# Attention scores of two heads at a time on the two row halves of the TensorE array

## The chip, the cores and the metric

One NeuronCore of one Trainium2 chip runs the kernel. The metric is the device time of one execution in microseconds (us); for the kernel before, three runs are given, and one more execution that the hardware profiler recorded.

## The reference

Attention with capped scores over 4 batches of 12 heads, 448 positions and 64 elements a head, then two blocks of dense products over the 1792 tokens.

```python
scale = 1.0 / np.sqrt(q.shape[-1])
scores = scale * np.matmul(q, k.transpose(0, 1, 3, 2))
scores = cap * np.tanh(scores / cap)
scores = scores - np.max(scores, axis=-1, keepdims=True)
attn = np.exp(scores)
attn = attn / (np.sum(attn, axis=-1, keepdims=True) + 1e-09)
attn_out = np.matmul(attn, v)
...
h = x @ w_in                      # 1792 x 768 x 2048
g = h * np.cos(h)
x = g @ w_out
a = x @ w1; b = x @ w2            # 768 x 1024
return ((a * b) @ w3) @ w_out2
```

## The kernel before, in words

The whole program is recorded first as a list of operations with due times (class `Plan`), and a planner then writes out every engine's order: at each moment it gives a free engine the ready operation with the earliest due time, by the costs that each operation names and the buffers that are free (`Ring`). The due times come from the table `PAR` (L294). What the planner sets is the order; on the chip the engines wait for one another by semaphores.

There are two copies of the program. The first, `columns` (L666), is the one that runs here; the other one (`general=True`) is entered only if the cap is over 40, and is not run with these inputs.

**Numbers in two parts.** Most products are made of values that are split into a high part and a low part of the type float32r, and three products (high by high, high by low, low by high; `mm3`, L380) are added in PSUM. A split is a cast for the high part and a subtraction for the low part (`copy` and `lo`).

**Scores.** Heads are taken in order, 48 of them, in steps `g`; a head has two steps (NT = 2), each for two of its four chunks of 112 keys, so there are 96 steps. For a pair of heads, `a_load` (L526) sends q and k of the two heads, each 64 rows by 2 × 448 columns, to SBUF twice: once to the upper 64 partitions and once to the lower 64. `a_split` (L540) makes from them `qh` and `ql` (high and low part of q, each on both halves of the partitions) and `ks`, whose upper 64 partitions hold the high part of k and whose lower 64 hold the low part. `c_S` (L605) then contracts over 128 rows: `ks` by `qh` (L612) and `ks` by `ql` (L613) give all four products of the parts with two matmuls a chunk. A step has four such matmuls of 448 columns, with weights of 112 columns, and fills the two banks of one `double`, of which there are two.

**The rest of attention.** `c_exp` (L617) takes tanh and exp of both banks in two ScalarE instructions a step. `c_PV` (L625) multiplies the result `p` by v in plain float32 (L633, each matmul shown as two instructions), with a half of the weights set to one so that the sums come out of the same product. `c_move`, `c_sums`, `c_norm` and `a_out` move, normalize and split the output.

**What stands around it.** While the scores go on, TensorE is given other products by due time: first `make_w34` (the product of w3 and w_out2, L381 to L383 on `w2h`, `w3h` and so on), then the units of the first dense block, `moe1` (on `xh`, `wih`, `g`, `woh`). After some 490 us no score products are left, and `moe1` and `moe2` fill the rest.

**Queues.** All DMAs are issued by SyncE (SP) in the planner's order. The first ones are the cap, q and k of the first pair, raw weights of w3 and w_out2, and v.

Of the kernel before, what the change touches and what calls it, by code (L numbers as in the profile page):

```python
# [11 lines left out]
F32 = mybir.dt.float32  # L12
F32R = mybir.dt.float32r
# [6 lines left out]
P = 128  # L20
B, H, S, D = 4, 12, 448, 64
CP = 112
NC = S // CP
# [6 lines left out]
NH = B * H  # L30
# [6 lines left out]
PAD = 64  # L37
# [97 lines left out]
class Plan:  # L135
# [156 lines left out]


PAR = dict(  # L294
    p1=3.4, p2=6.2, gsw=48, t0=10.0,
    ql=6, qs=3,
    hsw=27,
    wb=(20.0, 90.0), we=(90.5, 170.5), e1=2.6, e2=15.1, e3=20.0,
    m0=184.3, ua=14, pa=21.4, pu=14.75,
    wlead=3.1,  # L300


    wACT=1.0, wDVE=1.0, wPOOL=1.0, tw=432.21, back=1.13,
    nq=1, nqh=2, nph=2, npl=2,
    nraw=3, nx=2, w3bufs=2, w2bufs=6,
)
# [1 line left out]
    p1=1.98, p2=2.86, gsw=90, t0=14.13, ql=10, qs=4, hsw=26, wb=(30.36, 107.61), we=(108.65, 207.54),  # L308
    m0=222.0, ua=13, pa=19.15, pu=14.2, nt=9, nph=3,
# [22 lines left out]
def program(  # L332
# [15 lines left out]
    PE, ACT, DVE, POOL, SP = nc.tensor, nc.scalar, nc.vector, nc.gpsimd, nc.sync  # L348
    G = dict(PAR, **GENERAL) if general else PAR
    plan = Plan()  # L350
# [4 lines left out]
    def copy(due, dst, src, n, on, psum=False):  # L355
        opts = {
            "A": ("ACT", (0.051 if psum else 0.094) + n / 1200, lambda: ACT.copy(dst(), src())),  # L357
            "D": ("DVE", 0.068 + n / (960 if psum else 1920), lambda: DVE.tensor_copy(dst(), src()))  # L358
            + (() if psum else (True,)),
            "P": ("POOL", 0.16 + n / 1200,  # L360
                  lambda: POOL.tensor_scalar(dst(), src(), 1.0, 0.0, op0=ALU.mult, op1=ALU.add)),
        }
        plan.op(due, [opts[e] for e in on], r=[src], w=[dst])

    def tt(due, dst, a, b, n, op, on="D", psum=False):
        opts = {
            "D": ("DVE", 0.068 + n / 960, lambda: DVE.tensor_tensor(dst(), a(), b(), op=op))  # L367
            + (() if psum else (True,)),
            "P": ("POOL", 0.158 + n / 480, lambda: POOL.tensor_tensor(dst(), a(), b(), op=op)),
        }  # L370
        plan.op(due, [opts[e] for e in on], r=[a, b], w=[dst])

    def lo(due, dst, src, hi, n, on="PD", psum=False):
        tt(due, dst, src, hi.view(lambda t: t.bitcast(F32)), n, ALU.subtract, on, psum)

    def dma(due, dst, src, r=(), w=(), kb=115, write=False):
        plan.op(due, [("SP", 0.66, lambda: SP.dma_start(dst(), src()))], r=r, w=w,  # L377
                kb=kb)
# [6 lines left out]
    MM = (S + 32) / 2400  # L385
# [10 lines left out]
    for name, kw in dict(const={}, xring={}, dram=dict(space=DRAM), psum=dict(space=PSUM), doubles=dict(space=PSUM), singles=dict(space=PSUM), attn={}, lp={},  # L396
                         wi=dict(side="right"), wp=dict(side="right"), yp=right, hp=right, mp=right, cv=right,
                         q2=right).items():
# [17 lines left out]
    class Scratch:  # L416
# [7 lines left out]
        def at(self, sub, pick=None):  # L424
            return Ref(self.item, sub, pick)
# [31 lines left out]
    if general:  # L457
        s_r, pt_r, pv_r, hy_r = Banks((0, 1)), Banks((2, 3)), Banks((4, 5)), Banks((6, 7))
    else:
        s_r, pv_r, hy_r = Doubles((0, 1)), Banks((4, 5)), Banks((6, 7))  # L460
# [14 lines left out]
    if general:  # L475
# [18 lines left out]
    xl_r = ring("xring", "xl", [P, KD, S], F32R, 2)  # L494
    xh, xl = {}, {}
    A = {}
    tiles = [
        ("qr", [P, 2, S], F32, G["nq"]), ("kr", [P, 2, S], F32, G["nq"]), ("qh", [P, 2, S], F32R, G["nqh"]),
        ("ql", [P, 2, S], F32R, G["nqh"]), ("ks", [P, 2, S], F32R, G["nqh"]), 
        ("x32", [P, S], F32, 1), ("xsh", [P, S], F32R, 1), ("xsl", [P, S], F32R, 1),  # L500
    ]
    if general:
        tiles += [
            ("vr", [CP, NC, D], F32, 2), ("vs", [CP, NC, 2, D], F32R, 3), ("t", [CP, S], F32, G["nt"]), ("sm", [CP, 2, NC], F32, 4),
            ("rs", [CP, 2, NC], F32, 3), ("rb", [P, S], F32, 1),
            ("ph", [CP, S], F32R, G["nph"]), ("pl", [CP, S], F32R, G["npl"]),
        ]
    else:
        tiles += [(f"v{j}", [CP, NC, 2, D], F32, 2) for j in range(2)]
        tiles += [("p", [CP, 2, S], F32, 3), ("xs", [P, S], F32, 4), ("rs", [P, S // D], F32, 2), ("rb", [P, S], F32, 1)]  # L510
    for tag, shape, dtype, n in tiles:
        A[tag] = ring("attn", tag, shape, dtype, n)

# [4 lines left out]
    qk, vt, st, sm, rs, rb, s_t, t_t, pt_t, ph_t, pv_t, x32 = ({} for _ in range(12))  # L518

    def rows(j):  # L520
        return lambda t: t[j * D:(j + 1) * D]
# [4 lines left out]
    def a_load(i, g):  # L526
        b, h = divmod(i, H)
        qk[i] = A["qr"].new(), A["kr"].new()
        for it, src in zip(qk[i], (q2, k2)):
            for j in range(2):  # L530
                r = it.at(j, rows(j))
                dma(at(g) if i else -99.0, r, lambda src=src: src[b, h // 2].rearrange("(i d) s -> d i s", i=2),
                    w=[r], kb=230)
# [6 lines left out]
    def a_split(i, g):  # L540
        q, k = (Ref(x) for x in qk.pop(i))
        qh, ql, ks = (A[x].ref() for x in ("qh", "ql", "ks"))
        copy(at(g), ks, k, 2 * S, "PAD")
        low = Ref(ks.item, None, rows(1))
        lo(at(g), low, k.view(rows(1)), low, 2 * S)
        copy(at(g), qh, q, 2 * S, "PAD")
        lo(at(g), ql, q, qh, 2 * S)
        for j in range(2):
            st[i + j] = qh[:, j], ql[:, j], ks[:, j]
# [23 lines left out]
    def of_head(f, lag, g, n):  # L573
        i, c = divmod(g - lag, n)
        if c == 0 and 0 <= i < NH:
            f(i, g)

    def of_pair(f, lag, g, n):
        i, c = divmod(g - lag, n)
        if c == 0 and 0 < i < NH and i % 2 == 0:  # L580
            f(i, g)

    def each(f, lag, g, n):
        if 0 <= g - lag < n * NH:
            f(*divmod(g - lag, n), g)
# [4 lines left out]

    NT = NC // 2

    def c_consts():
        for j in range(2):
            r = A[f"v{j}"]
            for _, k in r.free:
                POOL.memset(r.tile(k)[:, :, 1 - j, :], 1.0)
# [4 lines left out]
        vt[i] = A[f"v{j}"].ref()  # L602
        dma(at(g), vt[i][:, :, j, :], lambda: v[b, h], w=[vt[i]])

    def c_S(i, c, g):  # L605
        qh, ql, ks = st[i]
        s = s_t[i, c] = s_r.ref()

        def f():
            for n in range(2):  # L610
                o, w = s()[:CP, n, :S], ks()[:, (2 * c + n) * CP:(2 * c + n + 1) * CP]
                PE.matmul(o, w, qh(), start=True, stop=False)  # L612
                PE.matmul(o, w, ql(), start=False, stop=True)  # L613

        plan.op(at(g), [("PE", 4 * MM, f)], r=st[i], w=[s])

    def c_exp(i, c, g):  # L617
        s = s_t.pop((i, c))[:CP, :, :S]
        p = ph_t[i, c] = A["p"].ref()
        for f, x, o in ((AF.Tanh, ts, s), (AF.Exp, pac, p)):  # L620
            plan.op(at(g), [("ACT", 0.144 + 2 * S / 1200,
                             lambda f=f, x=x, o=o: ACT.activation(o(), s(), f, scale=x[:CP]))],  # L622
                    r=[s], w=[o], table="exp")

    def c_PV(i, c, g):  # L625
        p = ph_t.pop((i, c))
        if c == 0:
            pv_t[i] = pv_r.ref()
        pv, w = pv_t[i], vt[i]

        def f():
            for n in range(2):
                PE.matmul(pv()[:, :S], w()[:, 2 * c + n].rearrange("p a d -> p (a d)"), p()[:, n, :],  # L633
                          start=c == 0 and n == 0, stop=c == NT - 1 and n == 1)

        plan.op(at(g), [("PE", 8 * MM, f)], r=[w, p], w=[pv])

    def c_move(i, g):
        pv, pv_t[i] = pv_t[i], A["xs"].ref()
# [25 lines left out]

    def columns():  # L666
        c_consts()
        a_load(0, -2)
        a_split(0, -1)
        for g in range(-8, NT * NH + 16):  # L670
            of_pair(a_load, -G["ql"], g, NT)
            of_head(cv_load, -2, g, NT)
            of_pair(a_split, -G["qs"], g, NT)
            each(c_S, 0, g, NT)
            each(c_exp, 0, g, NT)
            each(c_PV, 2, g, NT)
            of_head(c_move, 4, g, NT)
            of_head(c_sums, 4, g, NT)
            of_head(c_norm, 8, g, NT)
            of_head(a_out, 9, g, NT)  # L680
            if g == NT * G["hsw"] + 4:
                plan.move(pv_r, hy_r, at(g))
        first = plan.move(s_r, hy_r, at(g), lambda k: ())
        plan.move(s_r, hy_r, at(g), lambda k: range(4), part_doubles, [first])
        plan.move(pv_r, hy_r, at(g))
# [593 lines left out]


    (queries if general else columns)()
    first = make_w34()
    moe2(moe1(*first))
# [50 lines left out]
```

## Time and profile before

| | |
|---|---|
| three runs | 1100.07, 1101.58, 1103.51 us |
| the profiled execution | 1101.39 us |
| its span, first to last instruction | 1099.6 us |
| matmul instructions | 5040 |
| VectorE, share of the span | 80% |
| ScalarE | 46% |
| GpSimd | 14% |
| DMA, mean over the span | 154 GB/s |

The span is what the profile's times are counted from and in; 1.8 us of the execution lie around it. A busy share is an average over stages that have different limits, and a matmul's recorded end is a model, so what a matmul costs is read from the starts of the matmuls after it.

### The profile page before, as it was taken

Reading aid. Unit: us, or ns where it says so; the run is one execution under the profiler, and the core shown is the slowest. Engines: PE = TensorE matmul, PEld = TensorE weight load, DVE = VectorE, ACT = ScalarE, POOL = GpSimd, SP = SyncE. Lnnn points to the kernel's source line nnn. Section 1 sums busy time; section 2 is a strip of 40 time slices with the busy share of each in tenths; the row PEclk is TensorE's granted clock in tenths of the full one; section 3 lists DMA queues with packets and bytes.
Section 4 is the critical chain, followed back from the end, with each engine's and each line's share of the span. In section 5 each row is a group of like instructions: output and inputs, shape, how many; then the busy total and the mean of one; then the engine's idle time right before and its main releaser. Section 6 shows DMA issues by size and latency. Waiting matters only on the chain.

```text
span 1099.6 us, 14038 instructions
## 1 busy us (share of the span) xinstructions
PE 1075.0 (98%) x5040; PEld 938.1 (85%) x5040; DVE 882.5 (80%) x1338; ACT 505.2 (46%) x663; POOL 157.2 (14%) x153
## 2 busy tenths in 40 slices
PE   5999999999999999999999999999999999999996
PEld 3777777778888888889999999998999999999996
DVE  6897758698899989868789977779899879667642
ACT  4887667787666566642244221113333236321121
POOL 2232120131331301101001200001223100000000
PEclk9999999999999999999999999999999999999998
DMA  8885875868756654525643521103655436321132
GB/s 234 222 216 157 226 203 158 227 202 235 199 168 204 173 179 145 176 83 183 226 157 95 165 63 58 58 15 121 234 187 201 143 102 228 113 88 58 58 108 82
DMA packets 95554, 169.04 MB, mean 154 GB/s; under 512 B 37362, under 2 KB 68850, under 8 KB 95474
## 3 DMA queue, kind: packets, MB, share of 16 engines
q1 hardware_dynamic: 95474, 168.05, 51.0%
q8 instruction: 41, 0.67, 0.3%
q14 instruction: 39, 0.32, 0.1%
HBM read 129.30 MB, written 38.62 MB: 153 GB/s over the span
## 4 chain that ended last, share of the span: by engine, by line
PE 83%; DVE 8%; DMA 5%; issue 1%; SPq 1%; POOL 0%; ACT 0%; DVEq 0%; POOLq 0%; ACTq 0%
PE bank L383 23%; PE bank L382 23%; PE bank L381 23%; PE bank L633 9%; PE double L613 2%; PE double L612 2%; DMA raw<-in_w_out 2%; DMA kr<-in_k 1%; DMA rb<-rs_d 1%; SPq L377 1%; DVE x L854 1%; DVE y L367 1%; DMA rs_d<-rs 1%; DVE w L367 1%; DVE x L858 1%
## 5 line engine op out<-in xcount | busy, mean ns | idle before, releaser
L633 PE MATMUL bank<-p,v 112*128 112x448 f32 x384 | 161.1, 542 | 0.4 <-issue 0.4
L381 PE MATMUL bank<-xh,wih 128*128 128x448 f32 x384 | 148.4, 387 | 0.0
L381 PE MATMUL bank<-g,woh 128*128 128x448 f32 x384 | 145.7, 380 | 0.9 <-DVE y L358 0.9
L382 PE MATMUL bank<-g,woh 128*128 128x448 f32 x384 | 139.2, 363 | 0.9 <-DVE g L367 0.9
L382 PE MATMUL bank<-xl,wih 128*128 128x448 f32 x384 | 139.3, 363 | 0.0
L383 PE MATMUL bank<-g,wol 128*128 128x448 f32 x384 | 139.3, 363 | 0.0
L383 PE MATMUL bank<-xh,wil 128*128 128x448 f32 x384 | 139.2, 363 | 0.0
L367 DVE TENSOR_TENSOR y<-bank,y 128x448 f32<-128x448 f32 x168 | 103.7, 619 | 43.5 <-PE bank L383 42.5
L357 ACT COPY hs<-bank 128x448 f32<-128x448 f32 x83 | 44.3, 534 | 199.0 <-PE bank L383 198.8
L622 ACT ACTIVATE double<-double,ts 112x896 f32<-112x896 f32 x96 | 94.0, 980 | 66.3 <-PE double L613 66.0
L633 PEld LDWEIGHTS bank<-p,v 112*128 112x128 f32 x384 | 72.5, 190 | 40.8 <-issue 38.1
L622 ACT ACTIVATE p<-double,pac 112x896 f32<-112x896 f32 x96 | 96.8, 1011 | 2.1
L612 PE MATMUL double<-qh,ks 128*112 128x448 f32 x192 | 73.7, 384 | 14.0 <-DVE ks L367 10.0
L382 PEld LDWEIGHTS bank<-xl,wih 128*128 128x128 f32 x384 | 72.2, 188 | 10.5 <-issue 5.2
L382 PEld LDWEIGHTS bank<-g,woh 128*128 128x128 f32 x384 | 72.1, 188 | 10.0 <-issue 3.7
L381 PEld LDWEIGHTS bank<-g,woh 128*128 128x128 f32 x384 | 71.9, 187 | 10.1 <-issue 2.4
L381 PEld LDWEIGHTS bank<-xh,wih 128*128 128x128 f32 x384 | 72.0, 187 | 9.9 <-issue 4.7
L383 PEld LDWEIGHTS bank<-g,wol 128*128 128x128 f32 x384 | 72.1, 188 | 4.3
L383 PEld LDWEIGHTS bank<-xh,wil 128*128 128x128 f32 x384 | 72.0, 188 | 4.3
L613 PE MATMUL double<-ql,ks 128*112 128x448 f32 x192 | 72.0, 375 | 0.0
L382 PE MATMUL bank<-ab,w34h 128*128 128x448 f32 x192 | 69.7, 363 | 0.0
L381 PE MATMUL bank<-ab,w34h 128*128 128x448 f32 x192 | 69.7, 363 | 0.0
(219 smaller groups left out, 2313.3 us busy)
## 6 DMA issues: line engine op xcount, KB each, us to landing
rawc<-in_w_out SPq DMA_DIRECT2D x16, 768.0 KB, 5.5
stq<-w_d SPq DMA_DIRECT2D x32, 384.0 KB, 3.7
qr<-in_q SPq DMA_DIRECT2D x48, 224.0 KB, 4.7
kr<-in_k SPq DMA_DIRECT2D x48, 224.0 KB, 4.7
rawc<-in_w_in SPq DMA_DIRECT2D x13, 768.0 KB, 5.8
raw<-in_w3T SPq DMA_DIRECT2D x16, 512.0 KB, 5.6
rawl<-in_w SPq DMA_DIRECT2D x10, 768.0 KB, 4.9
raw<-in_w_out SPq DMA_DIRECT2D x8, 768.0 KB, 7.0
```

What stands on the lines that cost most here:

```text
L357: "A": ("ACT", (0.051 if psum else 0.094) + n / 1200, lambda: ACT.copy(dst(), src())),
L367: "D": ("DVE", 0.068 + n / 960, lambda: DVE.tensor_tensor(dst(), a(), b(), op=op))
L377: plan.op(due, [("SP", 0.66, lambda: SP.dma_start(dst(), src()))], r=r, w=w, kb=kb)
L381: PE.matmul(out, wh, xh, start=first, stop=False, skip_group_check=on)
L382: PE.matmul(out, wh, xl, start=False, stop=False, skip_group_check=on)
L383: PE.matmul(out, wl, xh, start=False, stop=last, skip_group_check=on)
L612: PE.matmul(o, w, qh(), start=True, stop=False)
L613: PE.matmul(o, w, ql(), start=False, stop=True)
L622: lambda f=f, x=x, o=o: ACT.activation(o(), s(), f, scale=x[:CP]))],
L633: PE.matmul(pv()[:, :S], w()[:, 2 * c + n].rearrange("p a d -> p (a d)"), p()[:, n, :], start=c == 0 and n == 0, stop=c == NT - 1 and n == 1)
L854: DVE.scalar_tensor_tensor(xi, h_(), 3, xi, op0=ALU.logical_shift_left, op1=ALU.bitwise_or)
L858: DVE.scalar_tensor_tensor(xi, l_(), 29, xi, op0=ALU.logical_shift_right, op1=ALU.bitwise_or)
```

## The change

For a pair of heads, q and k are now loaded once (`c_load`): head 0 of the pair stands on partitions 0 to 63, head 1 on 64 to 127, 448 columns each. `c_split` makes `kh`, `kl`, `qh` and `ql`, each of 128 partitions by 448 columns. A step is now one chunk of 112 keys for both heads: for each of three products (high by high, high by low, low by high) a matmul of 64 rows for head 0 and one for head 1, so six a step, where the fourth product (low by low) is no longer made. Head 0 writes the first bank of a `double`, head 1 the second. `c_PV` takes two chunks of one head from two tiles `p`, of which there are now six. The due times in `PAR` move.

```diff
 PAR = dict(
-    p1=3.4, p2=6.2, gsw=48, t0=10.0,
+    p1=3.2, p2=6.0, gsw=48, t0=7.5,
...
-    wb=(20.0, 90.0), we=(90.5, 170.5), e1=2.6, e2=15.1, e3=20.0,
-    m0=184.3, ua=14, pa=21.4, pu=14.75,
+    wb=(18.0, 83.0), we=(83.5, 158.5), e1=2.6, e2=15.1, e3=20.0,
+    m0=172.2, ua=14, pa=20.7, pu=14.75,
...
-    wACT=1.0, wDVE=1.0, wPOOL=1.0, tw=432.21, back=1.13,
+    wACT=1.0, wDVE=1.0, wPOOL=1.0, tw=410.0, back=1.13,
...
-        tiles += [("p", [CP, 2, S], F32, 3), ("xs", [P, S], F32, 4), ("rs", [P, S // D], F32, 2), ("rb", [P, S], F32, 1)]
+        tiles += [(x, [P, S], F32, G["nq"]) for x in ("qr", "kr")]
+        tiles += [(x, [P, S], F32R, G["nqh"]) for x in ("qh", "ql", "kh", "kl")]
+        tiles += [("p", [CP, 2, S], F32, 6), ("xs", [P, S], F32, 4), ("rs", [P, S // D], F32, 2), ("rb", [P, S], F32, 1)]
...
+    def c_load(i, g):
+        b, h = divmod(i, H)
+        qk[i] = A["qr"].ref(), A["kr"].ref()
+        for r, src in zip(qk[i], (q2, k2)):
+            dma(at(g) if i else -99.0, r, lambda src=src: src[b, h // 2], w=[r], kb=230)
+
+    def c_split(i, g):
+        st[i // 2] = []
+        for src, names in zip(reversed(qk.pop(i)), (("kh", "kl"), ("qh", "ql"))):
+            hi, low = (A[x].ref() for x in names)
+            copy(at(g), hi, src, S, "PAD")
+            lo(at(g), low, src, hi, S)
+            st[i // 2] += [hi, low]
...
-    def c_S(i, c, g):
-        qh, ql, ks = st[i]
-        s = s_t[i, c] = s_r.ref()
+    def c_S(n, c, g):
+        kh, kl, qh, ql = st[n]
+        s = s_t[n, c] = s_r.ref()
+        terms = (kh, qh), (kh, ql), (kl, qh)
 
         def f():
-            for n in range(2):
-                o, w = s()[:CP, n, :S], ks()[:, (2 * c + n) * CP:(2 * c + n + 1) * CP]
-                PE.matmul(o, w, qh(), start=True, stop=False)
-                PE.matmul(o, w, ql(), start=False, stop=True)
-
-        plan.op(at(g), [("PE", 4 * MM, f)], r=st[i], w=[s])
+            for k, (w, x) in enumerate(terms):
+                for j in range(2):
+                    r = slice(j * D, (j + 1) * D)
+                    PE.matmul(s()[:CP, j, :S], w()[r, c * CP:(c + 1) * CP], x()[r], start=k == 0, stop=k == 2)
+
+        plan.op(at(g), [("PE", 3 * MM, f)], r=st[n], w=[s])
...
-    def c_PV(i, c, g):
-        p = ph_t.pop((i, c))
-        if c == 0:
+    def c_PV(i, k, g):
+        n, j = divmod(i, 2)
+        ps = [ph_t[n, c] for c in (2 * k, 2 * k + 1)]
+        if k == 0:
             pv_t[i] = pv_r.ref()
         pv, w = pv_t[i], vt[i]
 
         def f():
-            for n in range(2):
-                PE.matmul(pv()[:, :S], w()[:, 2 * c + n].rearrange("p a d -> p (a d)"), p()[:, n, :],
-                          start=c == 0 and n == 0, stop=c == NT - 1 and n == 1)
+            for c, p in enumerate(ps):
+                PE.matmul(pv()[:, :S], w()[:, 2 * k + c].rearrange("p a d -> p (a d)"), p()[:, j, :],
+                          start=k == 0 and c == 0, stop=k == NT - 1 and c == 1)
...
-            each(c_PV, 2, g, NT)
-            of_head(c_move, 4, g, NT)
-            of_head(c_sums, 4, g, NT)
-            of_head(c_norm, 8, g, NT)
-            of_head(a_out, 9, g, NT)
+            if 0 <= g - 3 < NT * NH:
+                c_PV(*divmod(g - 3, NT), g)
+            of_head(c_move, 5, g, NT)
+            of_head(c_sums, 5, g, NT)
+            of_head(c_norm, 9, g, NT)
+            of_head(a_out, 10, g, NT)
```

The planner's orders show what moves. On TensorE, a step of the scores in the middle of `make_w34`; names are tiles with their buffer numbers, `bank_75` to `bank_78` are PSUM banks, and "x2" marks two instructions alike in a row. Before:

```order
L383 MATMUL bank_78<-w2h_261,w3l_175 128x384
L612 MATMUL double_82<-qh_128,ks_135 112x448
L613 MATMUL double_82<-ql_131,ks_135 112x448
L612 MATMUL double_82<-qh_128,ks_135 112x448
L613 MATMUL double_82<-ql_131,ks_135 112x448
L633 MATMUL bank_75<-p_161,v_107 128x448 x2
L381 MATMUL bank_78<-w2h_286,w3h_163 128x384
```

and in the changed kernel:

```order
L383 MATMUL bank_77<-w2h_298,w3l_172 128x384
L628 MATMUL double_82<-qh_127,kh_132 112x448 x2
L628 MATMUL double_82<-ql_129,kh_132 112x448 x2
L628 MATMUL double_82<-qh_127,kl_135 112x448 x2
L649 MATMUL bank_76<-p_157,v_113 128x448
L649 MATMUL bank_76<-p_170,v_113 128x448
L381 MATMUL bank_78<-w2h_266,w3h_161 128x384
```

Four matmuls of a step have become six, two (one a head) in each row that ends with "x2", and the neighbours are of the same kinds. In both orders the score products stand in 91 unbroken runs, 89 of one step, one of three steps and one, at the very start, of four, with other products before and behind each.

On VectorE, the splits ahead of the first score product. Before:

```order
L358 CAST qh_128<-qr_115 128x896
L367 TENSOR_TENSOR ql_131<-qr_115,qh_128 128x896
L358 CAST ks_135<-kr_118 128x896
L367 TENSOR_TENSOR ks_135<-kr_118,ks_135 64x896
L854 SCALAR_TENSOR_TENSOR x_147<-raw_121,x_147 128x512
```

and in the changed kernel:

```order
L358 CAST qh_127<-qr_115 128x448
L367 TENSOR_TENSOR ql_129<-qr_115,qh_127 128x448
L358 CAST kh_132<-kr_117 128x448
L367 TENSOR_TENSOR kl_135<-kr_117,kh_132 128x448
L873 SCALAR_TENSOR_TENSOR x_153<-raw_119,x_153 128x512
```

The same four instructions stand there in the same order, with half of the columns; the one that made the low part of k on 64 partitions now makes it on 128.

## Rows read from the trace of the kernel before

**Rows 1.** The page, part 1: busy time (share of the span) and instructions.
```profile
PE 1075.0 (98%) x5040; PEld 938.1 (85%) x5040; DVE 882.5 (80%) x1338; ACT 505.2 (46%) x663; POOL 157.2 (14%) x153
```

**Rows 2.** Windows: length, busy us of each engine (instructions), TensorE clock, DMA share, GB/s.
```profile
0.00:20.00 20.00, 8.01 (x20) 5.58 (x20) 11.81 (x17) 8.24 (x10) 6.32 (x13) 1.00 0.94 232
20.00:170.00 150.00, 147.52 (x632) 113.18 (x632) 115.60 (x164) 112.24 (x143) 31.60 (x34) 0.99 0.76 201
170.00:320.00 150.00, 149.09 (x646) 118.67 (x645) 130.70 (x182) 108.28 (x128) 33.72 (x28) 1.00 0.72 200
320.00:470.00 150.00, 150.00 (x667) 123.90 (x666) 134.38 (x199) 96.19 (x106) 26.71 (x25) 1.00 0.58 179
```

**Rows 3.** Waits of TensorE: total us, times, longest us.
```profile
PE double L612 <- DVE ks L367: 10.0, 1, 10.0
PE double L612 <- ACT p L622: 4.1, 2, 2.1
PE bank L382 <- DVE g L367: 0.9, 1, 0.9
PE bank L381 <- DVE y L358: 0.9, 1, 0.9
```

**Rows 4.** Groups of instructions, score matmuls: busy us, mean ns, idle before.
```profile
L612 PE MATMUL double<-qh,ks 128*112 128x448 f32 x192 | 73.7, 384 | 14.0 <-DVE ks L367 10.0
L613 PE MATMUL double<-ql,ks 128*112 128x448 f32 x192 | 72.0, 375 | 0.0
```

**Rows 5.** Timeline, TensorE matmuls, 298.5 to 301 us: start, length, instruction.
```profile
298.73 0.36 PE L612 MATMUL double<-qh,ks 128*112 128x448 f32 x1
...
299.33 0.37 PE L613 MATMUL double<-ql,ks 128*112 128x448 f32 x1
299.54 1.67 PE L633 MATMUL bank<-p,v 112*128 112x448 f32 x4
```

**Rows 6.** Timeline, weight loads around the wait that ends at 31.24 us.
```profile
28.60 0.17 PEld L613 LDWEIGHTS double<-ql,ks 128*112 128x112 f32 x1
31.24 0.17 PEld L612 LDWEIGHTS double<-qh,ks 128*112 128x112 f32 x1 [2.46 <-ACT p L622]
31.33 0.18 PEld L613 LDWEIGHTS double<-ql,ks 128*112 128x112 f32 x1
```

**Rows 7.** Timeline, the matmuls at the same place.
```profile
28.60 0.37 PE L612 MATMUL double<-qh,ks 128*112 128x448 f32 x1
...
31.24 0.46 PE L612 MATMUL double<-qh,ks 128*112 128x448 f32 x1 [2.06 <-ACT p L622]
31.54 0.37 PE L613 MATMUL double<-ql,ks 128*112 128x448 f32 x1
```

**Rows 8.** Timeline of the start, all engines, 0 to 21 us.
```profile
1.19 1.38 SPq L377 DMA_DIRECT2D qr<-in_q  x2
2.62 1.26 SPq L377 DMA_DIRECT2D kr<-in_k  x2
...
5.69 0.63 DVE L358 CAST qh<-qr 128x896 fp32r<-128x896 f32 x1 [1.40 <-DMA qr<-in_q]
...
8.18 0.63 DVE L358 CAST ks<-kr 128x896 fp32r<-128x896 f32 x1 [0.74 <-DMA kr<-in_k]
8.85 1.09 DVE L367 TENSOR_TENSOR ks<-kr,ks 64x896 fp32r<-64x896 f32 x1
...
9.99 0.71 PE L612 MATMUL double<-qh,ks 128*112 128x448 f32 x1 [9.99 <-DVE ks L367]
```

**Rows 9.** Groups of instructions of VectorE, shapes apart: subtractions of the splits.
```profile
L367 DVE TENSOR_TENSOR ks<-kr,ks 64x896 fp32r<-64x896 f32 x24 | 27.2, 1132 | 0.7
L367 DVE TENSOR_TENSOR ql<-qr,qh 128x896 fp32r<-128x896 f32 x24 | 26.6, 1110 | 0.4
```

**Rows 10.** Tile `xsh`, a split of 448 columns: ns min/median/max, first and last start.
```profile
L367 DVE TENSOR_TENSOR xsl<-x,xsh x11: 609/617/776, 241.6 to 514.8; 128x448 fp32r<-128x448 f32 x11
L358 DVE CAST xsh<-x x7: 385/387/1028, 238.8 to 438.8; 128x448 fp32r<-128x448 f32 x7
```

More of the change, by code (lines that the diff above doesn't have):

```diff
@@ L496, in program @@
     A = {}
[L497 to L501, printed above, removed]
+    tiles = [("x32", [P, S], F32, 1), ("xsh", [P, S], F32R, 1), ("xsl", [P, S], F32R, 1)]
     if general:
+        tiles += [(x, [P, 2, S], F32, G["nq"]) for x in ("qr", "kr")]
+        tiles += [(x, [P, 2, S], F32R, G["nqh"]) for x in ("qh", "ql", "ks")]
         tiles += [
@@ L603, in cv_load, with c_exp @@
         dma(at(g), vt[i][:, :, j, :], lambda: v[b, h], w=[vt[i]])
-    def c_S(i, c, g):
-        qh, ql, ks = st[i]
-        s = s_t[i, c] = s_r.ref()
+    def c_S(n, c, g):
+        kh, kl, qh, ql = st[n]
+        s = s_t[n, c] = s_r.ref()
+        terms = (kh, qh), (kh, ql), (kl, qh)
         def f():
-            for n in range(2):
-                o, w = s()[:CP, n, :S], ks()[:, (2 * c + n) * CP:(2 * c + n + 1) * CP]
-                PE.matmul(o, w, qh(), start=True, stop=False)
-                PE.matmul(o, w, ql(), start=False, stop=True)
-        plan.op(at(g), [("PE", 4 * MM, f)], r=st[i], w=[s])
-    def c_exp(i, c, g):
-        s = s_t.pop((i, c))[:CP, :, :S]
-        p = ph_t[i, c] = A["p"].ref()
+            for k, (w, x) in enumerate(terms):
[3 more added lines that the diff above has]
+        plan.op(at(g), [("PE", 3 * MM, f)], r=st[n], w=[s])
+    def c_exp(n, c, g):
+        s = s_t.pop((n, c))[:CP, :, :S]
+        p = ph_t[n, c] = A["p"].ref()
         for f, x, o in ((AF.Tanh, ts, s), (AF.Exp, pac, p)):
@@ L631, in f @@
         def f():
-            for n in range(2):
-                PE.matmul(pv()[:, :S], w()[:, 2 * c + n].rearrange("p a d -> p (a d)"), p()[:, n, :],
-                          start=c == 0 and n == 0, stop=c == NT - 1 and n == 1)
-        plan.op(at(g), [("PE", 8 * MM, f)], r=[w, p], w=[pv])
+            for c, p in enumerate(ps):
+                PE.matmul(pv()[:, :S], w()[:, 2 * k + c].rearrange("p a d -> p (a d)"), p()[:, j, :],
+                          start=k == 0 and c == 0, stop=k == NT - 1 and c == 1)
+        plan.op(at(g), [("PE", 8 * MM, f)], r=[w, *ps], w=[pv])
     def c_move(i, g):
@@ L667, in columns @@
         c_consts()
-        a_load(0, -2)
-        a_split(0, -1)
+        c_load(0, -2)
+        c_split(0, -1)
         for g in range(-8, NT * NH + 16):
-            of_pair(a_load, -G["ql"], g, NT)
+            of_pair(c_load, -G["ql"], g, NT)
             of_head(cv_load, -2, g, NT)
-            of_pair(a_split, -G["qs"], g, NT)
-            each(c_S, 0, g, NT)
-            each(c_exp, 0, g, NT)
-            each(c_PV, 2, g, NT)
-            of_head(c_move, 4, g, NT)
-            of_head(c_sums, 4, g, NT)
-            of_head(c_norm, 8, g, NT)
-            of_head(a_out, 9, g, NT)
-            if g == NT * G["hsw"] + 4:
+            of_pair(c_split, -G["qs"], g, NT)
+            if 0 <= g < NT * NH:
+                n, c = divmod(g, NC)
+                c_S(n, c, g)
+                c_exp(n, c, g)
+            if 0 <= g - 3 < NT * NH:
[4 more added lines that the diff above has]
+            of_head(a_out, 10, g, NT)
+            if g == NT * G["hsw"] + 5:
                 plan.move(pv_r, hy_r, at(g))
```

## The prediction

> **What bounds the kernel now.** I read the page's busy shares first: TensorE is busy for 98% of the span [rows 1]. That share alone proves little, since the ends of matmuls are modelled, so I read the windows next [rows 2]: from 20 to 470 us, the part that holds all score products, TensorE has 147.5, 149.1 and 150.0 us of work in each 150, while VectorE, the next busiest, has 116 to 134. The waits say the same [rows 3]: all that TensorE waited for another engine in the whole program is 10.0 us for the first `ks`, 4.1 us in two early waits for ScalarE's `p`, and two waits of 0.9 us. After the start nothing holds TensorE up but its own queue. So a score product that becomes cheaper shortens the program by that much, one that becomes dearer lengthens it, and work taken off the other engines buys nothing after the start.
>
> The groups of instructions give the scores 192 matmuls on L612 and 192 on L613 [rows 4]. Their means of 384 and 375 ns are not their price, because one starts before the record of the last has ended. The timeline has the price: the four matmuls of one step start at 298.73 us and the work behind them at 299.54 [rows 5], so 0.81 us for four, **0.202 us each**. The 384 cost 384 × 0.202 = **77.6 us**. A profiled execution took 1101.4 us (span 1099.6 and 1.8 around it); the median of the three runs is 1101.6, so sums made against the one hold for the other.
>
> **The change, part by part.** *Scores.* Four matmuls of 128 rows a step become six of 64 rows, on the upper and the lower half of the array by turns. The trace has no matmul on half of the array, so the price is bounded. Below: the two halves work at the same time, a pair costs one period of 0.202, and 288 pairs cost 58.2 us. Above: they do not, and 576 × 0.202 = 116.4 us. Which it is hangs on three things, each with a row or the lack of one.
>
> First, whether the second half may start while the first streams. Nothing here shows it; a full-array matmul always waits for the one ahead. I take it that it may, since the two share neither rows of the array nor a bank (each head of a pair has its own bank of `double`).
>
> Second, the weights: each of the six has its own load of 112 columns, and two of them must fit into 0.202 us. A weight load's record lasts 0.17 us, which would not fit twice. But after the wait that ends at 31.24 us the second load starts at 31.33 [rows 6], and the first matmul there, listed at 31.24, has its successor at 31.54 [rows 7]: 0.30 us, which is one period of 0.202 behind a load of 0.095. So two loads need 0.19 us and fit, by 0.01 us. Serial loads by the record's length would make a pair 0.35 us; I take the 0.095, because it is a spacing of starts and not a modelled end.
>
> Third, the edges of a run of score products. The order of the changed kernel has 91 such runs, as before, 89 of them of one step. In a stream a load starts with the matmul ahead of it (28.60 in [rows 6] beside 28.60 in [rows 7]). If that holds for the halves too, the second half of a run starts one load, 0.095 us, behind the first, and stays behind: half of the array is idle for 0.095 us at the run's start and the other half at its end. A run of one step then takes 3 × 0.202 + 0.095 = 0.70 us instead of 0.81, and all take 58.2 + 91 × 0.095 = 66.8 us. The bounds of an edge are 0 (both loads done before the run) and, on each side, the 0.16 us by which a matmul's record of 0.36 outlasts its period. I take 0.095 a run, the nearest row: **77.6 − 66.8 = 10.8 us saved**.
>
> The Trainium skill ("TensorE: Matmul & The Clock Gate", Part 3: Packing small matmuls) says that a weight load for another row group is pulled ahead of matmuls in flight and that matmuls on different row groups start about 4 ns apart; no run here shows it yet. By that rule the 91 edges vanish and the sum would be 8.6 us better: the first rival.
>
> *Loads of q and k.* Each pair had two copies of q and of k sent, one for each half of the partitions; now one. SP issues 48 DMAs less and half of the bytes go. They lie beside other work after the start, at no price. At the start they are on the path: both pieces of q are there by 5.69 us, k by 8.18, and the first matmul runs at 9.99 [rows 8]. With half of the bytes both should be there when q alone was, about 5.7 us. Behind that stand the splits, now 448 columns wide: a cast of 0.387 and a subtraction of 0.617 us [rows 10] where 0.63 and 1.09 stood [rows 8]. If q's two are done before k lands, the first matmul runs at 5.7 + 1.0 = 6.7 us, if not at 7.7: 3.3 or 2.3 us earlier. The weights of the next stage are queued behind these DMAs and move up as well. I take **2.7 us**, bounds 0 (another early chain sets the pace) and 3.3.
>
> *Splits in the steady part.* VectorE's 48 subtractions on `ks` and `ql` take 27.2 + 26.6 us [rows 9] and become 48 of 0.617 [rows 10], 29.6 us; the casts halve too. TensorE's own queue hides this; it only removes the danger that VectorE (134 of 150 us in the fullest window [rows 2]) becomes the bound when TensorE gets faster. If the relief were not there, TensorE's 2 to 3% would still leave VectorE under its limit.
>
> *PV and the due times.* PV has the same matmuls; one now waits for the `p` of two steps, and `p` has six buffers for three. A PV is queued a step later, with weight products and the next scores ahead of it, so nothing waits. The moved due times shift the fillers' order and leave their amount: nothing.
>
> **Sum:** 1101.4 − 10.8 − 2.7 = 1087.9, say **1088 us**. With an edge between 0.05 and 0.15 us this case runs from 1083 to 1093.
>
> **The rivals.** *1, both halves start together.* The lower half's load has a free place while the full-array matmul ahead streams, so it can be done before the run, and there is no edge. Scores 58.2 us, saved 19.4: 1101.4 − 19.4 − 2.7 = **1079.3 us**. For it: two loads take 0.19 us and the last full matmul gives 0.202. Against it: in the trace every load in a stream waits for the start of the matmul ahead [rows 6, 7]. By the rule of the skill given above, this is how it goes.
>
> *2, the array empties at each change between full and half, and the kernel is slower.* Each run has a change at both ends, 181 in all. If the next matmul waits until the last one is out of the array, each costs the 0.36 − 0.20 = 0.16 us of [rows 5]: 29.0 us, against 19.4 saved. 1101.4 + 9.6 − 2.7 = **1108.3 us**. It decides from (19.4 + 2.7) / 181 = 0.122 us a change on. For it: runs are short, three pairs between changes. Against it: the trace changes from 128 to 112 rows (PV) without a gap (0.21 us, [rows 5]), but both use the full array, so this speaks little. The Trainium skill ("TensorEngine Tiling (Array Packing)", Key Properties) states such a rule: to change the tiling mode drains TensorE; it gives no price, and no row here shows one.
>
> *3, a half's weights cannot load while that half computes.* Then load and product alternate in each half, a pair takes 0.095 + 0.202 = 0.297, all 85.5 us: 1101.4 + 7.9 − 2.7 = **1106.6 us**. Against it: in the full array load and product do overlap [rows 6, 7].
>
> *4, the change does not do what it says:* the halves run one after the other. 1101.4 + 38.8 − 2.7 = **1137.5 us**.
>
> **How the numbers follow.** A measurement of this kernel can tell about 0.3%, 3.3 us, from no change. The forecast's case gets 0.34, rival 1 0.30, rival 2 0.16 (with smaller prices of a change among them), rival 3 0.10, rival 4 0.10. Faster: 0.32 of the first, all of rival 1 and 0.02 of rival 2, 0.64. Within 0.3%: 0.02, 0.03 of rival 2 and 0.01 of rival 3, 0.06. Slower: the rest, 0.30. The range goes from rival 1 with the best start, 1077, to the price of rivals 2 and 3 with a small wait added, 1112; rival 4 and the far ends lie outside.
>
> **What would show it.** Right: the starts of the two heads' matmuls lie about 0.1 us apart and six take 0.70 us up to the next product; the first matmul stands at 6.7 to 7.7 us; TensorE's waits after the start stay under some 2 us. Rival 1 shows pairs that start together every 0.20 us; rival 2 a gap before the first and behind the last product of each run; rival 3 pairs every 0.30 us; rival 4 six starts 0.20 us apart. The forecast is wrong too if TensorE now waits for VectorE or for a landing in the middle of the scores.

## The result and the profile after

The changed kernel takes **1110.45 us** (median of five runs, 1109.11 to 1110.78) where the kernel before takes 1101.58 (five runs, 1100.07 to 1103.51): a ratio of 1.0076 with an interval of [1.0059, 1.0092]. It is slower by about 9 us; faster by 13 was forecast. The profiled execution took 1110.45 us, its span is 1108.6.

The windows of the profile after (columns as in [rows 2]) say that TensorE is still the engine that has no time left:

```profile
20.00:170.00 150.00, 147.75 (x698) 99.36 (x696) 100.63 (x167) 108.48 (x143) 23.38 (x28) 1.00 0.56 165
170.00:320.00 150.00, 150.00 (x684) 105.79 (x683) 120.38 (x184) 99.52 (x115) 33.04 (x29) 1.00 0.58 175
320.00:470.00 150.00, 150.00 (x696) 113.38 (x696) 123.28 (x190) 85.97 (x96) 26.47 (x28) 1.00 0.49 150
```

VectorE has become lighter, from 116, 131 and 134 us to 101, 120 and 123. So nothing that feeds TensorE has grown into the bound, and TensorE's waits for other engines (total us, times, longest us) are few, as in [rows 3]:

```profile
PE double L628 <- ACT p L637: 6.3, 4, 3.8
PE double L628 <- DVE kh L358: 6.0, 1, 6.0
PE bank L382 <- DVE g L367: 0.9, 1, 0.9
```

Both long ones lie in the first 32 us. Where the time went is seen in the starts of the same product in both programs. The answers for the tiles `w2h`, `yA11h` and the scores (instruction, count: ns min/median/max, first and last start in us) are, before,

```profile
L381 PE MATMUL bank<-w2h,w3h x128: 332/336/689, 23.4 to 193.5; 128*128 128x384 f32 x128
L381 PE MATMUL bank<-yA11h,xh x48: 360/363/368, 773.5 to 1043.7; 128*128 128x448 f32 x48
```

and after

```profile
L381 PE MATMUL bank<-w2h,w3h x128: 332/441/690, 21.1 to 195.1; 128*128 128x384 f32 x128
L381 PE MATMUL bank<-yA11h,xh x48: 362/363/363, 784.4 to 1054.6; 128*128 128x448 f32 x48
L628 PE MATMUL double<-qh,kh x192: 449/457/713, 6.0 to 490.6; 64*112 64x448 f32 x192
```

The changed kernel is ahead by 2.3 us when the first weight product runs (21.1 against 23.4) and behind by 10.9 when the second block begins (784.4 against 773.5); from there on the distance is constant (1054.6 against 1043.7). It lost some 13 us while there were score products, at the engine that makes them.

One run of score products shows how. This is TensorE's timeline of the changed kernel around 302 us (start, length, instruction), first the matmuls, then the weight loads:

```profile
302.32 0.36 PE L383 MATMUL bank<-g,wol 128*128 128x448 f32 x1
302.61 0.46 PE L628 MATMUL double<-qh,kh 64*112 64x448 f32 x2
302.91 0.37 PE L628 MATMUL double<-ql,kh 64*112 64x448 f32 x2
303.13 0.37 PE L628 MATMUL double<-qh,kl 64*112 64x448 f32 x2
303.43 1.02 PE L649 MATMUL bank<-p,v 112*128 112x448 f32 x2
```

```profile
302.13 0.19 PEld L383 LDWEIGHTS bank<-g,wol 128*128 128x128 f32 x1
302.61 0.17 PEld L628 LDWEIGHTS double<-qh,kh 64*112 64x112 f32 x2 [0.30 <-issue]
302.71 0.18 PEld L628 LDWEIGHTS double<-ql,kh 64*112 64x112 f32 x2
302.92 0.17 PEld L628 LDWEIGHTS double<-qh,kl 64*112 64x112 f32 x2
303.42 0.30 PEld L649 LDWEIGHTS bank<-p,v 112*128 112x128 f32 x2 [0.33 <-DVE y L367]
```

Inside the run all is as good as it could be: each row with "x2" is a pair, one product a half, listed as one since they start together, and pairs follow one another after 0.20 us. Even the two weight loads of a pair run at the same time. The ends are what costs. Before the run, the last full-array product starts at 302.32 and would be through its 0.20 us at 302.52; yet the first load of the run starts at 302.61, not beside that product as loads in a stream do [rows 6, 7], and the first pair streams one load later, from about 302.71 (its successor stands at 302.91). That is 0.19 us lost. Behind the run, the last pair starts at 303.13, its 0.20 us end at 303.33, PV's load starts only at 303.42 and PV streams from about 303.53, one load of 128 columns (0.11 us) later: 0.20 us lost. A run of one step costs 3 × 0.20 + 0.19 + 0.20 = 0.99 us where four full matmuls cost 0.81 [rows 5].

The other runs are alike: leaving out the first two, the median distance from start to start is 0.290 us in front of a run and 0.294 behind it, where the kernel before has 0.197 and 0.203. Over all, at 0.19 us an end, 91 × 0.38 = 34.6 us are lost at the ends, and 77.6 − 58.2 = 19.4 are won inside: by this count, 15.2 us more for the scores. This is where the forecast's sum broke. What stays open until something else is tried is whether the ends alone are the cause, and what the rest of the change is worth.

### The profile page after: what moved, and what is told of

It is laid out like the page before. It is cut to its first block, busy times and chain, and to the rows that moved or that the text cites. A ratio compares the mean times of both kernels' runs of the same rounds, so it can differ in the third digit from the quotient of the medians.

```text
span 1108.6 us, 14342 instructions
## 1 busy us (share of the span) xinstructions
PE 1088.9 (98%) x5232; PEld 907.5 (82%) x5232; DVE 854.9 (77%) x1352; ACT 489.6 (44%) x649; POOL 146.6 (13%) x153
## 4 chain that ended last, share of the span: by engine, by line
PE 96%; DVE 2%; ACT 1%; DMA 1%; issue 0%; SPq 0%; ACTq 0%
PE bank L381 25%; PE bank L382 25%; PE bank L383 25%; PE bank L649 14%; PE double L628 7%; DMA raw<-in_w3T 1%; DVE y L367 1%; DVE w L367 0%; DVE xl L367 0%; ACT p L637 0%; ACT raw L860 0%; ACT double L637 0%; DVE g L367 0%; DVE w L1002 0%; DVE kk L1007 0%
## 5 line engine op out<-in xcount | busy, mean ns | idle before, releaser
L649 PE MATMUL bank<-p,v 112*128 112x448 f32 x384 | 166.8, 558 | 0.0
L357 ACT COPY hs<-bank 128x448 f32<-128x448 f32 x76 | 40.5, 533 | 207.9 <-PE bank L383 207.9
L649 PEld LDWEIGHTS bank<-p,v 112*128 112x128 f32 x384 | 68.2, 191 | 57.4 <-issue 52.3
L383 PE MATMUL bank<-ab,w34l 128*128 128x448 f32 x192 | 69.3, 361 | 0.0
L381 PE MATMUL bank<-w2h,w3h 128*128 128x384 f32 x128 | 59.8, 467 | 0.0
```

Source lines behind the costliest of these rows:

```text
L381: PE.matmul(out, wh, xh, start=first, stop=False, skip_group_check=on)
L383: PE.matmul(out, wl, xh, start=False, stop=last, skip_group_check=on)
L649: PE.matmul(pv()[:, :S], w()[:, 2 * k + c].rearrange("p a d -> p (a d)"), p()[:, j, :], start=k == 0 and c == 0, stop=k == NT - 1 and c == 1)
```

## The experiments

Theory A says that TensorE loses 0.19 us, with the load that cannot be made ahead, whenever it goes from products on 128 rows to products on 64 rows or back. Theory B says that the ends are cheap and the loss lies in the rest of the change: order, PV, due times. Theory C says that the ends come from the two halves waiting for each other.

**The rest of the change without halves** (run full).

```diff
-            for k, (w, x) in enumerate(terms):
-                for j in range(2):
-                    r = slice(j * D, (j + 1) * D)
-                    PE.matmul(s()[:CP, j, :S], w()[r, c * CP:(c + 1) * CP], x()[r], start=k == 0, stop=k == 2)
+            for j in range(2):
+                for k, (w, x) in enumerate(terms[:2]):
+                    PE.matmul(s()[:CP, j, :S], w()[:, c * CP:(c + 1) * CP], x(), start=k == 0, stop=k == 1)
...
-        plan.op(at(g), [("PE", 3 * MM, f)], r=st[n], w=[s])
+        plan.op(at(g), [("PE", 4 * MM, f)], r=st[n], w=[s])
```

> The changed kernel with its scores made of four matmuls a step on all 128 rows (this sums the two heads' scores and leaves the product of k's low part out); loads, splits, PV and due times stay those of the change. Theory A: the changed kernel loses at the two ends of each of its 91 runs of half-array products, about 0.19 us an end. Its scores then cost 58.2 + 91 x 0.38 = 92.8 us where 77.6 stood, so all the rest of the change is worth 9.0 - 15.2 = -6.2 us, and this kernel, with scores at 77.6 us, takes 1095 us. Theory B: pairs are cheap and the ends too, and the loss lies in the rest (order, PV, due times). Scores then save 19.4 us in the changed kernel, the rest costs 28.4, and this kernel takes 1130 us.

Measured: 1096.78 us (1096.64 and 1096.92) beside 1102.34 for the kernel before on the same chip, a ratio of 0.9949 [0.9928, 0.9969]. Theory B, at 1130, is out. The rest of the change is worth 5.6 us *less* time; the halves alone cost 1110.45 − 1096.78 = 13.7 us, give or take the 0.8 us by which the kernel before differs between the two sets of runs (1101.58 and 1102.34). That is 1.5 us less than the count of 15.2; 1.3 us of waits for VectorE between 200 and 270 us, which this run has and the changed kernel has not, go that way. By the starts of `yA11h`,

```profile
L381 PE MATMUL bank<-yA11h,xh x48: 362/363/363, 770.9 to 1041.1; 128*128 128x448 f32 x48
```

2.6 us of the 5.6 are there by 771 us, which is the shorter start. The next 1.9 us of the difference lie behind TensorE's last product: its record ends 8.3 us before the end of the span in the kernel before, 6.4 us in this one. The instructions there are the same and the last output is on its way; why it is faster is open. The remaining 1.1 us are within what executions of the kernel before differ by (1100.46 to 1103.94).

**Only the upper half** (run upper): the same four products a step on rows 0 to 63 alone. The edit is shown against the kernel with full rows.

```diff
-                    PE.matmul(s()[:CP, j, :S], w()[:, c * CP:(c + 1) * CP], x(), start=k == 0, stop=k == 1)
+                    PE.matmul(s()[:CP, j, :S], w()[:D, c * CP:(c + 1) * CP], x()[:D], start=k == 0, stop=k == 1)
```

> As the kernel with full rows, but its four matmuls a step use the 64 rows of the upper half alone (scores of the second head are replaced by the first head's, and k's low part is left out). The number of matmuls and their length are the same, only the rows differ, so the difference of the two kernels is the price of the ends. Theory A (any change between 128 and 64 rows empties the array): 91 x 0.38 = 34.6 us more than with full rows, about 1130 us, and a gap at the end of every run though no product uses the lower half. Theory C (the loss comes from the two halves waiting for each other): no ends, about 1095 us.

Measured: 1131.83 us in one execution, 35.1 more than with full rows. In the program nothing differs between the two but the number of rows (and the values that come of it), and no product uses the lower half, so theory C is out: the change of the rows' number has the price, 35.1 / 91 = 0.39 us a run. A part of this is the start: at 42 us the kernel is 4.1 us behind after only four runs. The 87 runs that follow cost 31.2 us up to the second block, 0.36 each. Its timeline (matmuls) has the same two ends around four products that follow one another at 0.20 us:

```profile
298.54 0.37 PE L383 MATMUL bank<-g,wol 128*128 128x448 f32 x1
298.84 0.45 PE L627 MATMUL double<-qh,kh 64*112 64x448 f32 x1
299.13 0.36 PE L627 MATMUL double<-ql,kh 64*112 64x448 f32 x1
299.33 0.36 PE L627 MATMUL double<-qh,kh 64*112 64x448 f32 x1
299.53 0.36 PE L627 MATMUL double<-ql,kh 64*112 64x448 f32 x1
299.82 0.64 PE L648 MATMUL bank<-p,v 112*128 112x448 f32 x1
```

The first and the last gap, 298.54 to 298.84 and 299.53 to 299.82, are 0.30 and 0.29 us from start to start where a stream has 0.20, and behind each of them one load stands open as well.

**Twice the runs** (run split).

```diff
...
-        plan.op(at(g), [("PE", 3 * MM, f)], r=st[n], w=[s])
+        plan.op(at(g), [("PE", 1 * MM, lambda: f((0,)))], r=st[n], w=[s])
+        plan.op((at(g) + at(g + 1)) / 2, [("PE", 2 * MM, lambda: f((1, 2)))], r=st[n], w=[s])
```

Here `f` takes the list of the terms that it issues.

> The changed kernel with each step's six products as two pieces, first pair and other two pairs, due half a step apart, so that the order has 177 runs of half-array products instead of 91; the work is the same. Theory A: 86 more runs x 0.38 = 32.7 us more than the changed kernel, about 1143 us. Theory B: about 1110 us.

Measured: 1146.28 us in one execution, 35.8 more than the changed kernel where 32.7 were expected. The excess lies at the start. At 36.4 us this run is 2.8 us behind the changed kernel at the same amount of work, with one additional run of score products so far. Behind a wait of 2.3 us for ScalarE its clock stood at half (1.2 GHz) from 29.1 to 35.9 us, the 0.50 in the row of this stretch,

```profile
29.10:35.90 6.80, 6.04 (x14) 3.55 (x16) 6.32 (x10) 4.27 (x6) 2.31 (x2) 0.50 0.60 173
```

and the changed kernel's profile has no such stretch there. The 85 additional runs after that cost 33.0 us, 0.39 each: direction and size are theory A's.

**Half of the runs** (run two): one block of products for two steps, into both doubles.

```diff
-        s = s_t[n, c] = s_r.ref()
+        cs_ = c, c + 1
+        ss = [s_r.ref() for _ in cs_]
...
+            for m, s in zip(cs_, ss):
+                for k, (w, x) in enumerate(terms):
+                    for j in range(2):
+                        r = slice(j * D, (j + 1) * D)
+                        PE.matmul(s()[:CP, j, :S], w()[r, m * CP:(m + 1) * CP], x()[r], start=k == 0, stop=k == 2)
 
-        plan.op(at(g), [("PE", 3 * MM, f)], r=st[n], w=[s])
+        plan.op(at(g), [(None, 0.0, None)], w=ss[:1])
+        plan.op(at(g), [("PE", 6 * MM, f)], r=st[n], w=ss)
...
-                c_S(n, c, g)
+                if c % 2 == 0:
+                    c_S(n, c, g)
                 c_exp(n, c, g)
```

The operation without an engine only takes the first double, so that one product block can take two of them.

> The changed kernel with two steps' products issued as one block of twelve, so that the order has 47 runs instead of 91; both doubles are filled at once. Theory A: 44 runs less x 0.38 = 16.7 us less than the changed kernel, about 1093.7 us, and faster than the kernel before by about 0.7%. Theory B: 1110 us, or more, because TensorE must find both doubles free before a block and could wait for ScalarE's exp.

Measured: **1090.18 us** (1088.92 to 1091.47) beside 1102.34 for the kernel before, a ratio of 0.9885 [0.9868, 0.9902]; 20.3 us less than the changed kernel where 16.7 were expected. It beats both kernels. Its timeline shows the six pairs of a block with one pair of ends:

```profile
295.88 0.37 PE L383 MATMUL bank<-g,wol 128*128 128x448 f32 x1
296.17 0.46 PE L632 MATMUL double<-qh,kh 64*112 64x448 f32 x2
296.47 0.37 PE L632 MATMUL double<-ql,kh 64*112 64x448 f32 x2
296.68 0.36 PE L632 MATMUL double<-qh,kl 64*112 64x448 f32 x2
296.88 0.36 PE L632 MATMUL double<-qh,kh 64*112 64x448 f32 x2
297.08 0.37 PE L632 MATMUL double<-ql,kh 64*112 64x448 f32 x2
297.28 0.38 PE L632 MATMUL double<-qh,kl 64*112 64x448 f32 x2
297.58 0.64 PE L654 MATMUL bank<-p,v 112*128 112x448 f32 x1
```

The wait that theory B feared, for both doubles, did not come: after the first 14 us TensorE waits for ScalarE no more, and the waits are even 3.1 us shorter than the changed kernel's. Of the 3.6 us by which the run beat its expectation, 2.2 are there at 31 us, where no run has been saved yet. From there to the second block, 44 runs less save 17.2 us, 0.39 each.

```profile
PE double L632 <- DVE kh L358: 6.0, 1, 6.0
PE double L632 <- ACT p L642: 3.2, 2, 3.1
```

Little of the 12.2 us against the kernel before comes from the halves, though. 5.6 are the rest of the change, as the run with full rows measured it. Of the 6.6 against that run, 3.1 are there at 31 us: this one waits less for ScalarE (3.2 us against 5.9), and it has no stretch at half clock (the other has two, of 3.4 us each). Another 2.8 come up to the second block, and 1.3 of these are the waits for VectorE named above. So 1.5 are left for the halves, and the count gives the same, 77.6 − 58.2 − 47 × 0.38 = 1.5. The last 0.7 of the 6.6 stay open.

**The order of the halves** (run headwise): all three products of the upper half first, then the three of the lower.

```diff
-            for k, (w, x) in enumerate(terms):
-                for j in range(2):
+            for j in range(2):
+                for k, (w, x) in enumerate(terms):
```

> The changed kernel with a step's six products in the order of the heads: the three of the upper half, then the three of the lower half, in place of by turns. The runs and their ends stay 91. If products of the two halves overlap only where they stand next to each other in the queue (matmuls start in the order of issue), one pair of a run overlaps and it lasts five periods instead of three: 96 x 2 x 0.202 = 38.8 us more than the changed kernel, about 1149 us. If the halves work independently of the order, 1110 us. If two halves never overlap, six periods, 1168 us.

Measured: 1113.44 us in one execution, far from 1149 and from 1168. The timeline lists pairs again, although the program's order has `kh`, `ql`, `kl` of the upper half ahead of the lower half's first product:

```profile
299.15 0.37 PE L383 MATMUL bank<-xh,wil 128*128 128x448 f32 x1
299.45 0.47 PE L628 MATMUL double<-qh,kh 64*112 64x448 f32 x2
299.75 0.36 PE L628 MATMUL double<-ql,kh 64*112 64x448 f32 x2
299.95 0.36 PE L628 MATMUL double<-qh,kl 64*112 64x448 f32 x2
300.24 0.64 PE L649 MATMUL bank<-p,v 112*128 112x448 f32 x1
```

So the expectation's own theory fell: the lower half does not wait behind the upper half's queue, and "by turns" buys nothing here. The 3.0 us above the changed kernel are not a price of the order: at the 50th product that is no score, at 40 us, this run is 2.7 us behind, and at the 4600th it is 3.1 behind. They come from the start, where this execution had its clock at half (1.2 GHz) from 29.3 to 36.1 us. The wait for ScalarE just around it, 1.5 us, is in both profiles (it ends at 30.0 here and at 30.1 in the changed kernel's); the stretch at half clock is in this one alone.

```profile
29.30:36.10 6.80, 6.10 (x16) 4.18 (x17) 6.42 (x11) 5.73 (x8) 2.24 (x2) 0.50 0.47 146
```

## Why the prediction was wrong

**The bound: right.** TensorE was the only engine without slack, before and after, and its work sets the end: the 13 us that it lost while there were score products, from 2.3 ahead to 10.9 behind, were not made up again up to its last product.

**The price inside a run: right.** The halves overlap, a pair costs one period of 0.20 us, and the loads fit. They fit for another reason than was given: the prediction had two loads one behind the other in 0.19 us; the trace has both of a pair at the same time (302.61, x2), so there is no tight spot at all.

**The edges of a run: wrong, and this is the step that failed.** The prediction took 0.095 us a run, the stagger of two loads as they stand in a stream of full products, because that row was the nearest. The runs show no stagger and 0.38 us a run: at each change between 128 and 64 rows the next load starts only after the last product's period, and the next product one load later. This is the gap of rival 2. That the array empties in it is a reading; the traces show starts, and the ends of matmuls are modelled. The bound that was set for an end, 0.16 us by the length of a matmul's record, was too low too: of the 0.19 us measured some 0.09 pass until the array takes a load again, and 0.10 are that load itself, which in a stream lies under the product ahead. Rival 2's point of decision held: 0.122 us a change, against 0.19. That its time, 1108.3, missed the result by only 2.2 us is partly luck: its changes are 5.6 us too cheap (29.0 against 34.6), and the rest of the change gained 5.6 us where it had 2.7. The prediction gave it a chance of 0.16 although the kernel has two changes for every three pairs. The Trainium skill ("TensorEngine Tiling (Array Packing)", Key Properties) states that changing the tiling mode drains TensorE. The traces agree that a change costs time, 0.19 us each, a price that the page does not give.

**Rival 1: half right.** Products of the two halves start together (302.61, x2). The Trainium skill ("TensorE: Matmul & The Clock Gate", Part 3: Packing small matmuls) has such matmuls about 4 ns apart, and the trace agrees: the pairs of the changed kernel start 3 ns apart in the median and 20 ns at the most. But the load that was to be pulled ahead of the full product was not: across a change it starts 0.09 us after that product's period has ended (302.61 behind 302.52).

**Rivals 3 and 4: out.** Loads overlap with products in a half, and the halves with each other.

**Loads and splits: right in size.** 2.7 us were forecast; the first weight product runs 2.3 us earlier and, with full rows, the second block begins 2.6 us earlier. The first score product runs at 6.03 us, before the forecast's 6.7 to 7.7, because it waits for `kh` alone and the subtraction that makes `kl` runs beside it; the sum had both ahead of it. The 48 subtractions take 15.0 + 14.7 us, 29.7 where 29.6 were forecast; what they buy by themselves was not tried. PV and the due times were put at nothing, and with full rows TensorE's lead over the kernel before is 3.0 us at 34 us and 2.6 at the second block, so next to nothing came of them there. The 1.9 us behind TensorE's last product stood in no term.

**The range.** The measured time lies in it because rivals 2 and 3 set its upper end, not by the forecast's own case. Two of its figures are off by the prediction's own terms: rival 1 with the best start gives 1101.4 − 19.4 − 3.3 = 1078.7, not 1077, and the case's lower end comes to 1084, not 1083.

## What to carry to other kernels

Half-array products are worth it by the length of an unbroken block of them, not by their number: here a pair saves 0.067 us against the full products that it replaces (0.81 / 3 − 0.20), an unbroken block costs 0.38 us at its two ends, so by this count it needs six pairs to break even. The changed kernel had three and lost 13.7 us; of what the one with six gained, 1.5 us are left for its halves. Longer blocks were not tried. Where they have to stand between full products, gather them in longer blocks first (here by filling two PSUM buffers at once), and count the blocks in the engine's order before pricing the products. A row that shows a resource in a steady stream does not bound what a change of mode costs: if no row shows the change, its bound has to include the work that the stream hides.

## What the runs showed of the hardware that was not expected

- A change between 128 and 64 rows costs TensorE about 0.19 us in either direction, also when only one half is used (0.36 to 0.39 us a run in the kernel with the upper half alone). A change from 128 to 112 rows does not: before, PV on 112 rows starts 0.21 us after the score product ahead of it [rows 5].
- Weight loads of the two halves run at the same time (302.61, x2), while two loads of the full array are 0.095 us apart at the least that the trace shows [rows 6].
- Matmuls of the two halves do not keep the program's order between the halves: in the kernel ordered by heads the lower half's first product starts with the upper half's first, ahead of two that were issued before it.
